# Another order for the start of a spectral-mixing and MoE kernel: weight loads behind a fold, spills on ScalarE's queue, step 0 earlier, a second warm-up, PSUM banks by name

## The chip, the cores and the metric

One core of a Trainium2 chip runs the whole kernel. The metric is the device time of one execution in microseconds (us), the median of several runs. The core has five engines that work beside each other, each through its own instructions in order: TensorE (PE; its weight loads are listed as PEld), VectorE (DVE), ScalarE (ACT), GpSimd (POOL) and SyncE (SP). SP computes nothing and issues DMAs; ScalarE issues some too. Each of the two has its own DMA queue, and both feed the same 16 DMA engines. Engines wait for each other and for DMAs through semaphores.

## The reference

```python
def _attn_ref(x):                       # x: (8, 3008, 256) float32
    X = np.fft.fft(x, axis=1)
    X = np.fft.fft(X, axis=2)
    return X.real.astype(np.float32)

def _moe_ref(x, w_in, w_out):           # w_in (256, 2048), w_out (2048, 256), float64
    h = x @ w_in
    g = h * (1.0 / (1.0 + np.exp(-1.702 * h)))
    return (g @ w_out).astype(np.float32)

x = _attn_ref(x).reshape(8 * 3008, 256); return _moe_ref(x, w_in, w_out)
```

A two-dimensional Fourier transform of each of 8 batches (its real part), then two matrix products with a sigmoid-weighted unit between.

## The kernel before, in words

The transform along the sequence (3008 = 47 * 64) is split into two stages of matrix products with tables of sines and cosines, `tab1` and `tab2`. The transform along the 256 columns is not done on the data: it is folded into `w_in` once, at the start (`fold_w`). What follows is `h`, its activation and the product with `w_out`, batch by batch, in 48 steps for each: a step is one (batch, block, half, p), with three blocks of transform rows, two halves of a block and eight pairs p of 128 rows of the hidden dimension, 16 steps a block.

**Start, batch 0 only.** x arrives in 48 rows and their mirror images: `load_first` on SP's queue and `load_mirror` on ScalarE's, four of each, in groups of four columns numbered 0 to 7 that arrive as the pairs (0, 7), (1, 6), (2, 5), (3, 4). DVE folds each group (`fold_first`, L310 and L312), PE mixes it into one PSUM bank (`mix_first`, L330, eight times), ScalarE copies the bank out to a buffer of `made` (L332). A buffer holds two mixes. `spill_first` (L336) writes the first 16 rows of a buffer to DRAM (`Td`) as soon as it is full, one DMA for each half c of the partitions; rows 16 to 48 follow later. `fill` (L358) reads `Td` back in the order that the second stage wants. `rotate` (PE into bank `psr`, ScalarE L365) mends one column, `stage2` (PE L378, DVE transposes L385) makes the tile `pq`, the operand of all steps of a block. So the first `pq` needs the last spill, then the fill, then `psr`.

**Weights.** `w_in` and `w_out` come as float64 in four chunks each of 1 MB (`load_in`, `load_out`), into a ring of three buffers, and are turned to float32 by hand: `sizes` (absolute value of the high word, ScalarE L429 or DVE L431), `clamp` (POOL L435), `low` (ScalarE L439), `high` (DVE L454 and L455), `finish_in` or `finish_out` (POOL L467 or L475). `bounds` is prepare, sizes, clamp and low together. `halved` (DVE L480, L481) adds and subtracts the halves of a chunk of `w_in`, and `fold_w` (PE L191 or L501 into `psw`, ScalarE L508) transforms the chunk. `first_row` (PE `psf`) and `nyquist` (PE `psn`) mend two rows.

**Steps 0 to 7** run by a hand-written list, `SCRIPT`: for each step `hidden` (PE `pa` and `pb`, ScalarE L552), then the entries of the step. `rows` (DVE L582, L587, L589) makes h of a step and frees the banks `pa` and `pb`, `activate` (ScalarE L593) the unit, `product` (PE `o`) the product with `w_out`. Steps 2n and 2n+1 of `hidden` use chunk n of `w_in`, and so do the products with `w_out`. From step 8 on another scheme with fewer products runs, the same in both kernels. `differences` (POOL L493) and `small_weights` (DVE L712) prepare its weights.

**What sets the order.** Each engine runs its instructions in the order in which the program names them. PSUM banks are handed out in turn from the list `spare`: a call takes the first name and puts it at the end, and PE waits where the bank's last reader isn't done. A DMA may also wait for an earlier one: eight completion semaphores serve all DMAs in turn. `warm` are matmuls without use that keep PE busy.

```python
spare = ["b0", "b1", "b2", "o2", "o3", "o4"]
```

Of the kernel before, what the change touches and what calls it, by code (L numbers as in the profile page):

```python
# [119 lines left out]
def kernel(ctx: ExitStack, tc, x, w_in, w_out, tab1, tab2, out):  # L120
# [213 lines left out]
    def spill_first(k, m0, m1, engines):  # L334
        for c, eng in enumerate(engines):
            eng.dma_start(out=view(Td[0], (NJ * m0 + 16 * c + 12 - 4 * k) * D, [NJ * D, m1 - m0], [1, 4 * D]),  # L336
                          in_=made[k][64 * c + m0:64 * c + m1].rearrange("p q d -> p (q d)"))
# [29 lines left out]
    def stage2(b, blk):  # L367
# [14 lines left out]
        for u in range(NU):  # L382
            for cs in range(parts):

                nc.vector.transpose(free(pq[:], cs * 512 + u * RUN, [256, 4 // parts], [NU * RUN, 4], [1, RUN]),  # L385
                                    free(ps[u][:], cs * 256, [128, 4 // parts], [32, 4], [1, 32]))
# [472 lines left out]
    made = rooms[:3] + [pqp.tile([128, 4, D], F32, tag="pq", name="e")[:]]  # L859
# [3 lines left out]

    nc.vector.memset(twos[:], 0.0)
    for lo, hi in (28, 32), (24, 28), (20, 24), (8, 12), (12, 20):
        nc.gpsimd.memset(xt[:, lo:hi, :], 0.0)
    nc.vector.memset(xt[:, 0:4, :], 0.0)
# [19 lines left out]
    load_in(0, nc.sync, ((0, 1), (1, 2)))  # L887
    nc.sync.dma_start(out=small[:, :CD + 4 * H], in_=tab2[:])
    load_in(1, nc.sync)
# [4 lines left out]
    for i, need in enumerate(((0, 7), (1,), (6,), (2,), (5,), (3,), (4,), ())):  # L894
        for g in need:
            fold_first(g)
        mix_first(i)
# [3 lines left out]
        if i % 2:  # L901
            spill_first(i // 2, 0, 16, (nc.sync, nc.scalar))
# [11 lines left out]
    load_out(0, nc.sync)  # L914
# [6 lines left out]
    sizes(in1, nc.vector)  # L921
    low(in1)
    for h0 in (0, 512):
        clamp(in1, h0, 512)
# [8 lines left out]
    halved(1)  # L933
# [7 lines left out]
    spare.append(spare.pop(0))  # L941
    high(out0)
    load_in(3, nc.sync)
    finish_out(0)
    fold_w(1)
# [11 lines left out]
    for t, c in ((1, 2), (3, 3)):  # L957
        at(t, load_out, c, nc.sync)
# [13 lines left out]
    for b in range(B):  # L972
# [26 lines left out]
        for blk in range(NBLK):  # L999
# [7 lines left out]
        [(prepare, in2), (low, in2), (nyquist, 0, 0), (rows, 0, ((sizes, in2, nc.vector), (clamp, in2)))],  # L1007
        [(first_row, 1), (activate, 0), (rows, 1), (high, in2), (finish, in2)],
        [(activate, 1), (rows, 2), (halved, 2)],
        [(product, 0, 0, None), (product, 1, 0, None), (bounds, out1), (activate, 2), (bounds, in3), (rows, 3), (activate, 3),  # L1010
         (fold_w, 2), (high, out1), (finish, out1), (high, in3), (finish, in3)],
        [(first_row, 2), (rotate, 0, 4, NG, nc.scalar.copy), (rows, 4), (halved, 3)],
# [103 lines left out]
```

## Time and profile before

| | |
|---|---|
| median of 3 runs | 1846.46 us (1846.12 to 1846.71) |
| profiled execution | 1845.24 us, span 1843.5 us |
| mean granted TensorE clock | 0.997 of full speed |
| ACT busy | 1139.4 us (62%) |
| POOL busy | 997.7 us (54%) |
| PE busy in the first 10 us, 10 to 20, 20 to 30, 30 to 40 | 7.44, 9.40, 8.09, 8.28 |
| DMA | 105.95 MB, mean 57 GB/s; 202 GB/s in the first 10 us, 277, 245 and 349 in the next three tens |

The profile is one execution taken by the hardware profiler. The span runs from the first to the last instruction; the execution's time has 1.7 us more around it. Busy times are per engine, and register, semaphore and DMA-issuing instructions don't count. "x<-y" names the tile written and the tile read; L336 is line 336 of the kernel before. SPq and ACTq are the engines' DMA issues. A line of the chain of waits has the start, the length and what it was. In a table of stretches, the granted clock stands behind the engines (1.00 is full speed).

### The profile page before, as it was taken

To read this page: it belongs to the slowest core of one execution; us is meant where nothing else is said; L and a number is where in the kernel's file an instruction comes from. 1 tells how busy PE (TensorE), PEld (TensorE's weight loads), DVE (VectorE), ACT (ScalarE), POOL (GpSimd) and SP (SyncE) were. 2 spreads that over 40 slices of the span, in tenths; PEclk is the share of its full clock that TensorE was granted. 3 is DMA by queue.
4 is the path that set the end of the run, shared out by engine and by line. 5 is a ranking of instruction groups with operands and counts; after the bars stand their busy time and mean duration, and the time that the engine had idled before them with its cause. 6 is when DMAs were issued, how large, how long until landed. Compare 5 with 4: busy or idle time off the path is not lost.

```text
span 1843.5 us, 55849 instructions
## 1 busy us (share of the span) xinstructions
PE 1826.2 (99%) x23650; PEld 1398.9 (76%) x23650; DVE 1479.1 (80%) x1930; ACT 1139.4 (62%) x2231; POOL 997.7 (54%) x1068
## 2 busy tenths in 40 slices
PE   8999999999999999999999999999999999999998
PEld 4677777777777777777777777777777877778776
DVE  6888788887888778877888778878888788878874
ACT  4666656666666666666666666666656666556663
POOL 3785555554656546564456644666446654444442
PEclk9999999999999999999999999999999999999999
DMA  8721331114211151211502115020241102100101
GB/s 276 189 70 26 90 65 28 55 32 106 43 48 40 35 112 30 61 35 45 111 13 73 33 50 97 23 72 26 75 74 28 29 26 59 28 19 13 23 19 24
DMA packets 150841, 105.95 MB, mean 57 GB/s; under 512 B 106197, under 2 KB 131799, under 8 KB 150032
## 3 DMA queue, kind: packets, MB, share of 16 engines
q1 hardware_dynamic: 147760, 100.33, 22.6%
q8 instruction: 186, 3.05, 0.7%
q10 hardware_dynamic: 2832, 2.05, 0.5%
q14 instruction: 63, 0.52, 0.1%
HBM read 65.07 MB, written 48.05 MB: 61 GB/s over the span
## 4 chain that ended last, share of the span: by engine, by line
PE 95%; POOL 2%; DMA 1%; DVE 1%; issue 0%; ACT 0%; ACTq 0%; DVEq 0%; POOLq 0%; SPq 0%
PE x L191 35%; PE o L191 26%; PE low L701 25%; PE o L701 4%; PE ps L268 2%; PE ps L378 1%; DMA xt<-in_x_dram 1%; PE po L191 0%; DMA big<-in_moe_w_in_dram 0%; PE psw L501 0%; POOL wo L475 0%; PE pa L191 0%; POOL wo L493 0%; POOL big L632 0%; DMA t<-Td 0%
## 5 line engine op out<-in xcount | busy, mean ns | idle before, releaser
L632 POOL TENSOR_TENSOR big<-big 128x256 f32<-128x256 f32 (+1 forms) x376 | 353.6, 940 | 785.7 <-ACT big L624 672.2
L191 PE MATMUL x<-pq,wcs 128*64 128x256 f32 (+1 forms) x6016 | 768.8, 376 | 1.5 <-ACT g L614 0.9
L191 PE MATMUL o<-big,wo 128*64 128x256 f32 (+1 forms) x4800 | 621.0, 375 | 0.5 <-DVE big L639 0.5
L191 PEld LDWEIGHTS x<-pq,wcs 128*64 128x64 f32 x6016 | 414.1, 137 | 181.4 <-issue 15.6
L614 ACT ACTIVATE g<-x 128x512 f32<-128x512 f32 (+1 forms) x376 | 221.7, 590 | 380.1 <-PE x L191 378.9
L191 PEld LDWEIGHTS o<-big,wo 128*64 128x64 f32 x4800 | 341.8, 137 | 146.8 <-DVE big L639 0.9
L633 POOL TENSOR_TENSOR big<-big 128x256 f32<-128x256 f32 (+1 forms) x376 | 411.2, 1094 | 0.0
L621 DVE TENSOR_TENSOR big<-g,x 128x512 f32<-128x512 f32 (+1 forms) x376 | 250.7, 667 | 183.6 <-ACT big L617 183.4
L602 ACT ACTIVATE x<-nb,af 128x256 f32<-128x256 f32 (+1 forms) x752 | 353.0, 469 | 70.1 <-DVE pq L385 57.0
L701 PE MATMUL low<-big 128*64 128x128 f32 (+1 forms) x5888 | 381.4, 270 | 0.0
L701 PEld LDWEIGHTS low<-big 128*64 128x64 f32 x5888 | 336.9, 137 | 28.2
L617 ACT ACTIVATE big<-x 128x512 f32<-128x512 f32 (+1 forms) x376 | 219.2, 583 | 122.2 <-PE x L191 112.2
L663 DVE TENSOR_TENSOR big<-big 128x1024 f32<-128x1024 f32 (+1 forms) x184 | 235.4, 1280 | 65.9 <-PE low L701 43.1
L624 ACT ACTIVATE big<-big 128x512 f32<-128x512 f32 (+1 forms) x376 | 231.6, 616 | 34.9 <-DVE big L621 32.6
L701 PE MATMUL low<-big,wo 128*64 128x128 f32 (+1 forms) x2944 | 220.3, 270 | 0.1
L665 DVE TENSOR_TENSOR big<-big 128x512 f32<-128x512 f32 (+1 forms) x184 | 179.6, 976 | 16.3 <-DVE big L663 0.5
L667 DVE TENSOR_TENSOR big<-big 128x512 f32<-128x512 f32 (+1 forms) x184 | 184.0, 1000 | 0.0
L701 PEld LDWEIGHTS low<-big,wo 128*64 128x64 f32 x2944 | 171.8, 137 | 4.2 <-DVE big L667 0.5
L640 DVE TENSOR_TENSOR big<-big 128x512 f32<-128x512 f32 (+1 forms) x188 | 143.3, 762 | 6.5
L639 DVE TENSOR_TENSOR big<-big 128x512 f32<-128x512 f32 (+1 forms) x188 | 131.2, 698 | 3.5 <-POOL big L632 3.5
L803 DVE TENSOR_TENSOR big<-big,low 128x512 f32<-128x512 f32 (+3 forms) x184 | 109.0, 609 | 3.8
L701 PEld LDWEIGHTS o<-big,wo 128*64 128x64 f32 x1472 | 92.3, 137 | 24.9
(104 smaller groups left out, 1100.5 us busy)
## 6 DMA issues: line engine op xcount, KB each, us to landing
out_dram<-os SPq DMA_DIRECT2D x284, 64.0 KB
t<-Td SPq DMA_DIRECT2D x22, 512.0 KB
Td<-xt SPq DMA_DIRECT2D x56, 192.0 KB
xt<-in_x_dram SPq DMA_DIRECT2D x14, 512.0 KB
xt<-Xr SPq DMA_DIRECT2D x14, 512.0 KB
nb<-Nd SPq DMA_DIRECT2D x23, 256.0 KB
out_dram<-os SPq DMA_DIRECT2D x96, 56.0 KB
Xr<-in_x_dram SPq DMA_DIRECT2D x7, 752.0 KB
```

Source lines behind the costliest of these rows:

```text
L191: nc.tensor.matmul(out[c0:c0 + 64], lhsT=lhs[:, c0:c0 + 64], rhs=rhs, skip_group_check=True, **how)
L602: nc.scalar.activation(x[:, i * 256:i * 256 + n], nbt[b, blk][:, hh * 256:hh * 256 + n], ACTF.Copy, scale=af1[:, f:f + 1])
L614: nc.scalar.activation(two(g[:], n), two(xb[t][:], n), ACTF.Copy, scale=2.0)
L617: nc.scalar.activation(front(t), two(xb[t][:], width(t)), ACTF.Gelu_apprx_sigmoid)
L621: nc.vector.tensor_tensor(back(t), two(gt.pop(t)[:], n), two(xb.pop(t)[:], n), op=ALU.subtract)
L624: nc.scalar.activation(back(t), back(t), ACTF.Gelu_apprx_sigmoid)
L632: eng.tensor_tensor(right(t, S1, n), left(t, A21, n), right(t, A22, n), op=ALU.add)
L633: eng.tensor_tensor(left(t, S3, n), left(t, A11, n), left(t, A21, n), op=ALU.subtract)
L663: nc.vector.tensor_tensor(free(big[:], SUM, *both_), free(big[:], from11 + w, *twice), free(big[:], from11, [at_right(t, 0) + w - from11, ...
L665: nc.vector.tensor_tensor(s2, a11, s1, op=ALU.subtract)
L667: nc.vector.tensor_tensor(s4, a12, s2, op=ALU.subtract)
L701: nc.tensor.matmul(o, lhsT=lhs, rhs=rhs, start=first_in, stop=(p == NP - 2), skip_group_check=True)
```

## The change

- `spill_first` can take several groups in one DMA. The first 16 rows of all buffers go on ScalarE's queue, behind mixes 1, 5 and 7 rather than 1, 3, 5 and 7, and the second and third buffer go together. To lie side by side, these two change places in `made`.
- The loads of `w_in`, chunks 0 and 1, and of `tab2` are issued by SP behind the fold of group 6 (the fourth fold, ahead of mix 2): a 4-byte store to DRAM reads what that fold wrote and stands ahead of them. `tab2` comes in two DMAs, the part for `fold_w` first. `load_out(0)` follows them at once; it stood behind the first `fill`.
- The sizes of `w_in`'s chunk 1 move from DVE (one instruction) to ScalarE (two halves).
- `halved(1)`, `high(out0)`, `load_in(3)`, `finish_out(0)` and `fold_w(1)` move from ahead of step 0 into step 0, behind its `hidden`. `stage2` transposes the cosine halves of both banks ahead of the sine halves.
- `warm(2)` stands ahead of `rotate`, and the banks from there on are named one by one in a list of 23.
- In `SCRIPT`, the entries of steps 0 to 3 are regrouped (chunk 2 of `w_in` is prepared over steps 0 to 2, chunk 3 is ahead of `w_out`'s chunk 1), and `load_out(2)`, `load_out(3)` stand behind the `high` that reads their buffer.
- One memset of x stands first on DVE.

```diff
-    def spill_first(k, m0, m1, engines):
+    def spill_first(k, m0, m1, engines, groups=1):
         for c, eng in enumerate(engines):
-            eng.dma_start(out=view(Td[0], (NJ * m0 + 16 * c + 12 - 4 * k) * D, [NJ * D, m1 - m0], [1, 4 * D]),
-                          in_=made[k][64 * c + m0:64 * c + m1].rearrange("p q d -> p (q d)"))
+            part = made[k][64 * c + m0:64 * c + m1]
+            eng.dma_start(out=view(Td[0], (NJ * m0 + 16 * c + 12 - 4 * k) * D, [NJ * D, m1 - m0], [1, 4 * groups * D]),
+                          in_=free(part, 0, [1, 4 * groups * D]))
...
-        for u in range(NU):
-            for cs in range(parts):
+        for cs in range(parts):
+            for u in range(NU):
...
-    made = rooms[:3] + [pqp.tile([128, 4, D], F32, tag="pq", name="e")[:]]
+    made = [rooms[0], rooms[2], rooms[1]] + [pqp.tile([128, 4, D], F32, tag="pq", name="e")[:]]
...
+    nc.vector.memset(xt[:, 0:4, :], 0.0)
     nc.vector.memset(twos[:], 0.0)
...
-    nc.vector.memset(xt[:, 0:4, :], 0.0)
...
-    load_in(0, nc.sync, ((0, 1), (1, 2)))
-    nc.sync.dma_start(out=small[:, :CD + 4 * H], in_=tab2[:])
-    load_in(1, nc.sync)
     warm(6)
...
+        if i == 2:
+            nc.sync.dma_start(out=Tk[0:1, :], in_=room[6][0:1, 0, 0:1])
+            load_in(0, nc.sync, ((0, 1), (1, 2)))
+            nc.sync.dma_start(out=small[:, CD:CD + 4 * H], in_=tab2[:, CD:])
+            nc.sync.dma_start(out=small[:, :CD], in_=tab2[:, :CD])
+            load_in(1, nc.sync)
+            load_out(0, nc.sync)
         mix_first(i)
...
-        if i % 2:
-            spill_first(i // 2, 0, 16, (nc.sync, nc.scalar))
+        if i in (1, 5, 7):
+            spill_first((0, 2, 3)[i // 3], 0, 16, (nc.scalar, nc.scalar), 1 + i % 3 // 2)
...
     fill(0, 0, 4)
-    load_out(0, nc.sync)
     load_in(2, nc.sync)
...
-    sizes(in1, nc.vector)
+    for h0 in (0, 512):
+        sizes(in1, nc.scalar, h0, 512)
+        clamp(in1, h0, 512)
     low(in1)
-    for h0 in (0, 512):
-        clamp(in1, h0, 512)
...
     fold_w(0)
-    halved(1)
+    spare[:] = ["b0", "o2", "b1", "b2", "b0", "o2", "o3", "o4", "b1", "b2", "o4", "o2", "b0", "o3", "b1", "b2", "b0", "b1", "o4", "o3",
+                "b2", "o2", "o4"]
+    warm(2)
     rotate(0, 0, 4, nc.scalar.copy)
...
     first_row(0)
-    spare.append(spare.pop(0))
-    high(out0)
-    load_in(3, nc.sync)
-    finish_out(0)
-    fold_w(1)
...
-    for t, c in ((1, 2), (3, 3)):
-        at(t, load_out, c, nc.sync)
...
     SCRIPT = (
-        [(prepare, in2), (low, in2), (nyquist, 0, 0), (rows, 0, ((sizes, in2, nc.vector), (clamp, in2)))],
-        [(first_row, 1), (activate, 0), (rows, 1), (high, in2), (finish, in2)],
-        [(activate, 1), (rows, 2), (halved, 2)],
-        [(product, 0, 0, None), (product, 1, 0, None), (bounds, out1), (activate, 2), (bounds, in3), (rows, 3), (activate, 3),
-         (fold_w, 2), (high, out1), (finish, out1), (high, in3), (finish, in3)],
-        [(first_row, 2), (rotate, 0, 4, NG, nc.scalar.copy), (rows, 4), (halved, 3)],
-        [(product, 2, 0, None), (activate, 4), (bounds, out2), (rows, 5), (activate, 5), (fold_w, 3), (high, out2), (finish, out2)],
+        [(nyquist, 0, 0), (halved, 1), (high, out0), (load_in, 3, nc.sync), (finish, out0), (prepare, in2),
+         (rows, 0, ((sizes, in2, nc.vector), (clamp, in2))), (fold_w, 1)],
+        [(activate, 0), (first_row, 1), (rows, 1)],
+        [(low, in2), (activate, 1), (high, in2), (load_out, 2, nc.sync), (finish, in2), (rows, 2)],
+        [(bounds, in3), (activate, 2), (prepare, out1), (sizes, out1, nc.scalar), (clamp, out1), (rows, 3), (activate, 3), (low, out1),
+         (halved, 2), (product, 0, 0, None), (product, 1, 0, None), (fold_w, 2), (high, in3), (finish, in3), (high, out1),
+         (load_out, 3, nc.sync), (finish, out1)],
+        [(first_row, 2), (rotate, 0, 4, NG, nc.scalar.copy), (halved, 3), (rows, 4)],
+        [(product, 2, 0, None), (activate, 4), (rows, 5), (bounds, out2), (fold_w, 3), (activate, 5), (high, out2), (finish, out2)],
...
-                spare[:] = [tag for tag in spare if tag[0] == "o"] + ["b2"]
+                spare[:] = ["o4", "o2", "o3", "b2"]
```

## The prediction

> **What bounds the kernel now.** The page first: PE is busy for 1826.2 of the span's 1843.5 us, and the chain that ended last is PE for 95%.
>
> ```profile
> PE 1826.2 (99%) x23650; PEld 1398.9 (76%) x23650; DVE 1479.1 (80%) x1930; ACT 1139.4 (62%) x2231; POOL 997.7 (54%) x1068
> ...
> PE 95%; POOL 2%; DMA 1%; DVE 1%; issue 0%; ACT 0%; ACTq 0%; DVEq 0%; POOLq 0%; SPq 0%
> ```
>
> From 100 to 1843 us PE is busy 1735.41 of 1743 us at full clock, and the change edits nothing there. So it can only shift the moment from which PE runs without gaps. The second view is the table of stretches over the start; its columns are the stretch, its length, the busy time of PE, PEld, DVE, ACT and POOL, the granted clock, the DMA share and GB/s.
>
> ```profile
> 22.00:26.00 4.00, 3.05 (x28) 1.56 (x25) 3.60 (x5) 2.40 (x5) 2.21 (x3) 1.00 0.92 362
> 26.00:28.00 2.00, 1.96 (x10) 0.48 (x8) 1.25 (x1) 1.19 (x1) 1.36 (x2) 1.00 0.03 10
> 28.00:30.00 2.00, 1.08 (x6) 0.14 (x2) 1.59 (x3) 1.17 (x2) 0.92 (x2) 1.00 0.49 89
> 30.00:32.00 2.00, 0.28 (x12) 0.29 (x17) 1.90 (x2) 0.00 (x0) 1.31 (x1) 0.97 1.12 440
> 32.00:36.00 4.00, 4.00 (x85) 2.82 (x86) 2.65 (x6) 2.07 (x3) 1.94 (x2) 0.50 0.99 378
> 36.00:40.00 4.00, 4.00 (x22) 1.68 (x20) 1.92 (x2) 2.08 (x7) 1.84 (x3) 0.66 0.75 274
> 59.00:61.00 2.00, 0.23 (x4) 0.00 (x0) 1.97 (x4) 0.58 (x1) 2.00 (x2) 1.00 1.02 383
> ```
>
> Three things are to be seen: the DMA engines are full until 26 and empty from 26 to 28; PE is idle around 30 and again at 59 to 61; and the clock is halved from about 31.9 (0.97 over two us) to about 38.7 (0.66 over four), nearly 7 us. Third, the chain of waits over the same place (start, length, what):
>
> ```profile
> 23.58 0.60 ACT e L332
> 24.20 3.17 DMA Td<-e
> ...
> 27.50 4.08 DMA t<-Td
> 31.59 0.14 issue
> 31.72 0.29 PE psr L191 x4
> 32.01 1.89 PE ps L378 x64
> 33.90 0.95 PE psf L191 x16
> 34.84 3.52 PE psw L501 x8
> 38.36 1.09 PE pa L191 x8
> ```
>
> The last spill of the first transform lands at 27.4, the read-back (`fill`) at 31.59, and only then can PE go on. From there PE is the chain. Last, what PE waits for between 24 and 100 us (total, times, longest):
>
> ```profile
> PE psr L191 <- DMA t<-Td: 2.6, 1, 2.6
> PE pb L191 <- DVE big L589: 1.9, 1, 1.9
> PE psw L191 <- POOL wst L467: 1.0, 1, 1.0
> PE pa L191 <- DVE big L589: 0.3, 1, 0.3
> ```
>
> **The change part by part**, in the profiled execution's time (span 1843.5, execution 1845.24; the median of the runs is 1846.46, so 1.22 are added at the end).
>
> *Weight loads behind the fold of group 6.* SP now waits for the DVE fold that starts at 15.00 and takes 0.69, then issues a 4-byte store (0.4), so the first `w_in` load is issued at about 16.1 instead of 14.92 (SP's timeline). Queued behind that wait on SP are both `w_in` loads, the tables and, new here, `load_out(0)`; the fill comes behind all of them. From issue to first data this queue took 2.0 us for that load and 1.3 for the fill, so weights flow from about 17.8. x's last pieces lose that rival: in the trace, the last fold that waits for x starts at 18.53. The gain for the folds is 0 to 1.0; I take 0.4. It doesn't reach the end of this stage, because ScalarE, which copies the results out, waits for the first `w_in` half (20.44 now, about 20 after) and now issues two spills of 0.36 each ahead of its last two copies, where it issued one. The last spills are issued at about 24.0 to 24.8 against 24.20: nothing.
>
> *Spills on ScalarE's queue behind a longer line of weights.* Bytes that must move from 17.8 on: 1.05 MB (w_in, chunk 0), 0.46 (tables), 1.05 (chunk 1), 1.05 (`load_out(0)`, formerly issued behind the fill at 27.93) and 0.52 of spills: 4.1 MB. The rows from 22 to 26 move 362 GB/s, the best slices inside them about 400. At 400 that is 10.3 us, so they end at 28.1, and 0.6 to 1.2 more pass until the slowest engine has counted its completion: the last spill lands at about 29.0 instead of 27.38. Bounds: it passes the weights because its queue is its own (about 27.1, by the 3.17 of the row above from an issue at 24.0), or comes behind everything at 362 GB/s (29.9). I take 29.0 for this reason: in this trace spills on ScalarE's queue did not pass. Issued at 19.63 and 22.70, they were complete at 24.94 and 27.06, 5.3 and 4.4 us later, among SP's spills issued at about the same times. Grouping two into one saves SP's and ScalarE's issue times (0.3 to 0.36 each), which hide in this wait. The fill then takes 4.08 with nothing ahead of it, as now: `psr` starts at about 33.2, **+1.5** (bounds -0.4 and +2.5).
>
> The Trainium skill (DMA: Bandwidth & Descriptors, "Queues, rings and completion order") has each DMA engine take turns between the queues packet by packet, by which the last spill would land near 27 and this term would be about -0.2. The two completions at 24.94 and 27.06 speak against that here.
>
> *Warm-up.* Two 128x512 matmuls (three took 2.84 at full clock, so 0.95 each) follow `fold_w(0)`, which ends at 29.1 once a bank is copied out: PE is busy to 31.0, then idle for 2.2 until `psr`. The trace has an idle of 2.64 (29.08 to 31.72), after which the clock fell, and one of 1.92 (59.23 to 61.15), at 1.00 throughout. 2.2 lies nearer to the second; I take it that the clock stays. The Trainium skill (TensorE: Matmul & The Clock Gate, "Why this matters for your kernels") asks for no idle over about 3 us. The 2.64 here shows that less is enough to lose the clock.
>
> *Step 0 ahead of `fold_w(1)`.* Before, from `psr` (31.72) to the end of step 1's `pb` (42.73) takes 11.0. After, at full clock: 0.2 and the second stage 1.1 (the same 64 rows took 1.19 at 84.10); hand-off 0.2; the first two of the four transposes 0.75, which the new loop order makes the ones `pa` needs, and which `psw` used to cover: 2.3. Then `pa`, `pb`, `psn` 0.87 each: 4.9; `psw` 1.72 (its row at 53.97): 6.6; `pa` 0.87: 7.5. Step 1's `pb` takes bank o2, which `rows(0)` frees. DVE gets there by the transposes (ready at 2.95), `halved(1)` 1.3, `high(out0)` 1.9, then L582, the sizes of in2, two L587 and L589 with 0.6 + 0.7 + 0.87 + 0.69: 9.0. So PE waits 1.5 and ends at 9.9: **-1.1**. With the clock halved, this part would lose about 1.8 (half of the 6.8 us, less what DVE's wait hides).
>
> *The waits behind it.* The 0.3 at 43.3 goes, since the banks are named so that `pa` of step 2 takes a free one: **-0.3**. The 1.9 at 59.2 is `pb` waiting for `rows(4)` to free its bank, with DVE behind a 2.18 us L455 that usually takes 1.23. The named bank removes the wait: at most -1.9. What is late next is the chain POOL finish, differences, clamp, DVE high and small weights, on the critical path from 59.97 to 85.9, while PE there has no gap. So part is given back: **-1.0** (bounds -1.9 and +1.4, the second from the rival below). `sizes(in1)` moves from DVE (1.25) to two ScalarE halves (0.7 each) ahead of the copies of `psw`, whose cover is the wait for the fill; `load_out(2)`, `load_out(3)` and `load_in(3)` change place behind DVE's `high`, which already released their buffers.
>
> Sum: +1.5 - 1.1 - 0.3 - 1.0 = -0.9, and -0.1 for the x memset put first on DVE: -1.0. 1845.24 - 1.0 + 1.22 = **1845.5**. A measurement of this kernel tells 0.2% (3.7 us) from no change.
>
> **The rivals.**
> *The clock falls all the same* in the idle before the late fill: -1.0 + 1.8 = +0.8, 1847.3. For it: 2.2 is also close to 2.64, and the second stage's small tiles may not count as work, since the clock stayed low through them from 32 to 36. Against it: the 1.92. Chance 0.25.
> *The spills pass the weights*, the engines taking the two queues in turn: the last lands near 27.1, the fill shares the engines with the rest of `load_out(0)`, and `psr` is at 31.5, so -1.0 - 1.7 = -2.7, 1843.8; with the whole 1.9 gained too, 1842.8. For it: the queue of spills holds nothing else by then. Against it: the two completions above. Chance 0.17.
> *POOL's finish of out1 is the new wait*, and the kernel ends slower. It now stands behind in3's finish: in3 2.36 and out1 3.85 in their slow rows, from about 56.2, end at 62.4, where PE would be ready for `product(2)` at 60.0. PE waits 2.4 and the 1.0 is lost: -1.0 + 3.4 = +2.4, 1848.9. It decides once that finish ends after about 61. Against it: at the usual 2.50, it ends at 61. Chance 0.10.
> *The change does nothing at the start* since the DMA total is the same: it isn't the same ahead of the fill, so this is within the first case.
>
> **How the numbers follow.** Forecast 0.48 (its own range 1843.8 to 1847.0, by the bounds of fill and later waits), clock 0.25, passing 0.17, POOL 0.10. Low end 1842.8, the passing case with the full gain; high end 1849.0, the POOL case, or a halved clock with the fill at +2.5. Over 3.7 us faster (below 1842.8) needs passing and every later gain: 0.10. Slower than 1850.2 needs two rivals together: 0.05. Within: 0.85.
>
> **What would show it.** Right: first `w_in` issue near 16.1; last spill landing near 29 and `psr` near 33; PEclk 1.00 from 32 to 40; 1.5 of PE idle before step 1's `pb` on L590 (the old L589); no idle of 1.9 near 59. Wrong: `psr` before 32 (spills pass), PEclk 0.5 after 33, or a wait of `o` on POOL's `wo` near 60. From 120 us on the two traces should keep one distance; if that grows, the cause is one I haven't named.

## The result, and the profile after

The changed kernel takes 1850.25 us (median of 17 runs, 1848.59 to 1851.61) against 1846.71 for the kernel before (17 runs beside it, 1845.42 to 1848.80): a ratio of 1.0018, 95% interval 1.0011 to 1.0026. It is 3.5 us slower, within the 0.2% that was called no change, but the interval leaves 1 out. The forecast was 1845.5, and 1850.25 lies above its range of 1842.8 to 1849.0.

The profiled execution took 1850.66 us with a span of 1848.6, so 5.1 more than the span of before. The page's first line and its chain:

```profile
PE 1828.8 (99%) x23654; PEld 1406.5 (76%) x23654; DVE 1480.1 (80%) x1929; ACT 1139.5 (62%) x2233; POOL 1000.2 (54%) x1068
...
PE 93%; DMA 2%; POOL 2%; DVE 1%; ACT 1%; issue 1%; SPq 0%; ACTq 0%; DVEq 0%; POOLq 0%
```

PE's share of the chain fell by 2 points, and DMA and ACT took some of it. The table of stretches over the start (stretch, length, busy time of PE, PEld, DVE, ACT and POOL, granted clock, DMA share, GB/s):

```profile
22.00:26.00 4.00, 3.62 (x44) 2.37 (x42) 3.93 (x6) 2.09 (x4) 2.19 (x3) 1.00 1.06 425
26.00:28.00 2.00, 1.84 (x8) 0.39 (x8) 0.40 (x1) 1.74 (x3) 0.97 (x1) 1.00 0.98 404
28.00:30.00 2.00, 1.64 (x8) 0.48 (x8) 1.05 (x2) 1.75 (x3) 1.46 (x3) 1.00 0.16 64
30.00:32.00 2.00, 2.00 (x6) 0.68 (x4) 1.97 (x3) 0.65 (x2) 1.31 (x1) 1.00 0.19 19
32.00:36.00 4.00, 1.43 (x53) 1.23 (x60) 0.47 (x1) 0.90 (x2) 1.26 (x1) 0.92 0.89 320
36.00:40.00 4.00, 4.00 (x60) 2.62 (x44) 3.21 (x7) 1.97 (x5) 1.04 (x1) 0.50 0.98 347
57.00:61.00 4.00, 2.88 (x20) 1.17 (x18) 3.03 (x2) 3.29 (x6) 3.70 (x2) 1.00 0.00 0
```

The DMA engines are now full until 28 instead of 26, and then nearly empty until 32: the pause of before is two us later and longer. PE is busy through 30 to 32, with the warm-up, but does 1.43 of the four us from 32. The clock is halved in 36 to 40 all the same. What PE waits for between 24 and 100 us:

```profile
PE psr L191 <- issue: 2.6, 1, 2.6
PE o L191 <- POOL wo L476: 1.6, 2, 1.1
PE x L191 <- ACT x L603: 1.4, 1, 1.4
PE pa L191 <- ACT wcs L509: 1.3, 2, 1.1
```

For `psr` the profile names no releaser ("issue"); by the time it is the fill, issued at 30.62. The 1.9 of `pb` on DVE and the 0.3 of `pa` are gone. In their place stand three waits on other engines, 4.3 us in sum. Adding up between moments that both traces have, in us (differences in the last column):

| | before | after | |
|---|---|---|---|
| `psr` starts | 31.72 | 34.78 | +3.06 |
| `psr` to `product(0)` | 15.34 | 15.07 | -0.27 |
| `product(0)` to `psw` of chunk 2 | 6.91 | 6.91 | 0 |
| `psw` of chunk 2 to `psw` of chunk 3 | 11.52 | 12.63 | +1.11 |
| `psw` of chunk 3 to the first `x` | 9.32 | 9.46 | +0.14 |
| first `x` to the 22000th PE row from the end | 83.83 | 85.40 | +1.57 |
| from there to the end of the span | 1684.86 | 1684.35 | -0.51 |

The sum is 5.1. The profiled execution of before (1845.24) lies 1.5 us under its median and that of after 0.4 above, so of the 5.4 between the two executions 3.5 are left between the medians. Two numbers of this table are used for every run below: the start of `psr`, and the way from `psr` to that 22000th row (126.92 before, 129.47 after), which says what the steps cost once the start is taken out.

### The profile page after: what moved, and what is told of

Its sections match the earlier page's. It is cut to its first block, busy times and chain, and to the rows that moved or that the text cites. A ratio compares the mean times of both kernels' runs of the same rounds, so it can differ in the third digit from the quotient of the medians.

```text
span 1848.6 us, 55856 instructions
## 1 busy us (share of the span) xinstructions
PE 1828.8 (99%) x23654; PEld 1406.5 (76%) x23654; DVE 1480.1 (80%) x1929; ACT 1139.5 (62%) x2233; POOL 1000.2 (54%) x1068
## 4 chain that ended last, share of the span: by engine, by line
PE 93%; DMA 2%; POOL 2%; DVE 1%; ACT 1%; issue 1%; SPq 0%; ACTq 0%; DVEq 0%; POOLq 0%
PE x L191 34%; PE o L191 26%; PE low L702 25%; PE o L702 4%; PE ps L268 2%; PE ps L379 1%; DMA big<-in_moe_w_in_dram 1%; DMA Td<-e 0%; DMA xt<-in_x_dram 0%; DMA wo<-in_tab_dram 0%; PE po L191 0%; POOL wo L476 0%; POOL wo L494 0%; POOL big L633 0%; DVE big L713 0%
## 5 line engine op out<-in xcount | busy, mean ns | idle before, releaser
L191 PE MATMUL o<-big,wo 128*64 128x256 f32 (+1 forms) x4800 | 627.8, 375 | 2.1 <-POOL wo L476 1.6
L191 PEld LDWEIGHTS x<-pq,wcs 128*64 128x64 f32 x6016 | 421.4, 137 | 178.1 <-issue 15.6
L191 PEld LDWEIGHTS o<-big,wo 128*64 128x64 f32 x4800 | 346.3, 137 | 147.4 <-POOL wo L476 2.6
L625 ACT ACTIVATE big<-big 128x512 f32<-128x512 f32 (+1 forms) x376 | 231.6, 616 | 37.0 <-DVE big L622 34.7
L702 PEld LDWEIGHTS low<-big,wo 128*64 128x64 f32 x2944 | 175.6, 137 | 3.9 <-DVE big L668 0.3
L702 PEld LDWEIGHTS o<-big,wo 128*64 128x64 f32 x1472 | 94.0, 137 | 24.3
```

Source lines behind the costliest of these rows:

```text
L191: nc.tensor.matmul(out[c0:c0 + 64], lhsT=lhs[:, c0:c0 + 64], rhs=rhs, skip_group_check=True, **how)
L625: nc.scalar.activation(back(t), back(t), ACTF.Gelu_apprx_sigmoid)
L702: nc.tensor.matmul(o, lhsT=lhs, rhs=rhs, start=first_in, stop=(p == NP - 2), skip_group_check=True)
```

## The experiments

Every kernel was timed against the kernel before on the same chip, in four groups of four; a ratio compares across groups better than a median. "Lists" is the kernel before with the new lists of the steps 1 to 5.

| edit | median us | ratio, 95% interval | `psr` | way |
|---|---|---|---|---|
| loads half only | 1847.78 | 1.0012, 1.0003 to 1.0020 | 34.29 | 126.78 |
| step half only | 1848.54 | 1.0015, 1.0005 to 1.0024 | 33.71 | 129.79 |
| after, memsets as before | 1849.27 | 1.0018, 1.0009 to 1.0027 | 35.16 | 128.04 |
| after, `load_out(0)` behind the fill | 1848.41 | 1.0013, 1.0004 to 1.0022 | 32.43 | 129.74 |
| before, spills only | 1845.48 | 0.9997, 0.9988 to 1.0006 | 32.53 | 127.90 |
| before, step 0 only | 1846.45 | 1.0001, 0.9992 to 1.0010 | 34.10 | 127.06 |
| before, lists of steps 1 to 5 only | 1850.99 | 1.0027, 1.0016 to 1.0038 | 31.97 | 132.66 |
| before, `warm(2)` only | 1845.69 | 0.9996, 0.9987 to 1.0005 | 33.34 | 127.91 |
| lists, out1 ahead of in3 | 1850.05 | 1.0020, 1.0011 to 1.0028 | 32.81 | 130.94 |
| after, out1 ahead of in3 | 1848.21 | 1.0012, 1.0004 to 1.0021 | 34.82 | 128.29 |
| after, out1 first, `load_out(0)` back | 1848.82 | 1.0013, 1.0005 to 1.0022 | 32.54 | 130.54 |
| before, spills and `warm(2)` | 1844.99 | 0.9996, 0.9987 to 1.0005 | 31.72 | 126.93 |
| lists, out1 first, `rows(4)` first | 1848.04 | 1.0009, 1.0000 to 1.0017 | 32.98 | 127.64 |
| after, `rows(4)` first | 1848.16 | 1.0011, 1.0002 to 1.0019 | 34.27 | 127.46 |
| after, steps 3 and 4 and `load_out(0)` as before | 1845.35 | 0.9994, 0.9986 to 1.0003 | 32.33 | 126.45 |
| before, spills, `warm(2)`, named banks | 1844.74 | 0.9994, 0.9985 to 1.0003 | 32.20 | 125.67 |

The last two columns are of one profiled execution each. When x's last pieces land varies by one or two us between executions, so a `psr` alone says less than the group of runs. In the seven kernels whose loads and first spills are those of before, `psr` starts between 31.72 and 34.10, mean 32.9, and the profile of before is the earliest of them. In the five with the loads and spills of the changed kernel it starts between 34.27 and 35.16, mean 34.7. By the groups the start is later by 1.7, not by the 3.06 of the one pair.

### The two halves

Each takes its lines of the change's diff, and leaves the others as before. *Loads half*: spills, loads behind the fold, memset, sizes of in1 (the diff down to `sizes(in1, nc.scalar, h0, 512)`, without the loop order in `stage2`). *Step half*: that loop order, `warm(2)`, named banks, step 0 and the lists.

> Only the loading half of the change: memset order, weight loads and load_out(0) behind the fold of group 6, spills on ScalarE's queue, sizes(in1) on ScalarE; the steps as before. Theory A (the loss is the late fill): psr near 34.8 against 31.72, and the whole loss is here, about +3 us against before (0 to +0.5 would refute it). Theory B (the loss is the new order of the steps): psr is as late, but the slack in the steps hides most of it: +1 us or less.

> Only the step half: transposes by cosine and sine, warm(2), named banks, halved(1), high(out0) and fold_w(1) inside step 0, the new lists of steps; the loads as before. Theory A: psr at 31.7 with no loss, 0 to -2 us against before, since warm(2) ends at about 31.0, the idle ahead of psr is under 1 us and the clock stays at 1.00. Theory B: PE still waits about 1.1 for ScalarE near 57, 1.7 for POOL near 62 and 1.3 for DVE near 88, and the kernel is +1 to +2 us slower than before.

Each half alone is slower: by 0.12% with a late `psr` (34.29) and the old way (126.78), and by 0.15% with a longer way (129.79). Both expectations missed in part. The loads half lost 1.7 us by the medians, between theory A's 3 and theory B's 1. The step half refutes theory A: it lost 2.5, a little above theory B's range, with waits of the kind that theory B names (2.4 on wcs, 0.9 on POOL, 1.3 on `x`), and the clock fell for 3.41 us behind an idle of 1.6. So two things had to be explained, a late start and dear steps.

### The late start: what stands ahead of the last spills

First the memset, whose new place also exchanges the completion semaphores: x's last load of `load_first` was issued at 11.62 in the changed kernel and at 7.98 before.

```diff
-    nc.vector.memset(xt[:, 0:4, :], 0.0)
     nc.vector.memset(twos[:], 0.0)
...
+    nc.vector.memset(xt[:, 0:4, :], 0.0)
```

> The changed kernel with the memset of x put back behind the others on DVE, nothing else. In the changed kernel x's last load on SP's queue was issued at 11.62 against 7.98 and landed at 19.56 against 16.40, because it now waits for the end of the table load. If the memset's place decides which earlier DMA it waits for: issue near 8, the last fold that waits for x about 1 us earlier, psr near 33.8 and about 1 us less than the changed kernel, +2.5 against before. If the DMA engines are the limit whatever the order: psr stays near 34.8 and +3.5 against before.

With the memsets back that load was issued at 7.81, but x's mirrors landed later instead (the last at 19.49) and `psr` came at 35.16. The order of x's loads isn't the cause; the DMA engines are full then.

Then `load_out(0)`:

```diff
-            load_out(0, nc.sync)
...
     fill(0, 0, 4)
+    load_out(0, nc.sync)
```

> The changed kernel with load_out(0) back behind the fill, nothing else. Theory A1 (spills wait behind all weights in one line): the last spill lands about 2 us earlier (28.3 against 30.48), psr near 32.7, 1.5 to 2 us less than the changed kernel. Theory A2 (the spills don't wait for load_out(0)): last spill and psr as in the changed kernel, 30.5 and 34.8, no gain.

`psr` came at 32.43, 2.35 earlier. The last two spills, issued at 25.07 and 25.42, landed at 27.83 and 27.98, under 2.8 us later. In the changed kernel this took 4.65 and 4.98. The other kernels agree: the last spill lands 4.8 to 5.2 us behind its issue in the five that have `load_out(0)` ahead of it, and 2.4 to 2.8 in the six that have the spills on ScalarE's queue and `load_out(0)` behind the fill. Two views of the changed kernel show it, SP's issues and the chain of waits (start, length, what):

```profile
15.92 0.83 SPq L412 DMA_DIRECT2D big<-in_moe_w_in_dram  x2
...
20.43 0.47 SPq L417 DMA_DIRECT2D big<-in_moe_w_out_dram  x1
30.62 0.38 SPq L359 DMA_DIRECT2D t<-Td  x1
```

```profile
25.15 0.31 ACTq L337
25.46 0.04 issue
25.50 4.97 DMA Td<-e
```

`load_out(0)` was issued 5 us ahead of the spills, and the fill (30.62) waited for the spills, which landed behind its megabyte. The spills on ScalarE's queue were tried by themselves, on the kernel before:

```diff
-    made = rooms[:3] + [pqp.tile([128, 4, D], F32, tag="pq", name="e")[:]]
+    made = [rooms[0], rooms[2], rooms[1]] + [pqp.tile([128, 4, D], F32, tag="pq", name="e")[:]]
...
-        if i % 2:
-            spill_first(i // 2, 0, 16, (nc.sync, nc.scalar))
+        if i in (1, 5, 7):
+            spill_first((0, 2, 3)[i // 3], 0, 16, (nc.scalar, nc.scalar), 1 + i % 3 // 2)
```

> The kernel before with one part of the change: the first spills all on ScalarE's queue, two groups in one DMA (and so the order of the made buffers). w_in, the tables and load_out(0) stay where they were (load_out(0) behind the fill), and the clock is not cared for. Theory A (of the loading half, load_out(0) ahead of the spills is what costs; the spills' new queue and form cost nothing): the fill is issued 2.4 to 3.2 us behind the last spill's issue, psr starts between 31.0 and 32.7, the time is 1845.5 to 1847.0, ratio 0.9995 to 1.0005. Rival B (one queue for all spills is itself the loss, for they land one behind the other): the last spill lands 4.5 us or more behind its issue with no load_out in its way, psr starts at 33.5 or later, the time is 1847.5 to 1848.5.

Here the last spill landed 2.5 us behind its issue (25.77 to 28.23), and the median came 1.1 below that of the kernel before, which the interval does not tell from 1. Theory A held, rival B fell.

But little of the 2.35 us came back as time: 1848.41, by the ratios 0.0005 (0.9 us) less than the changed kernel, with a way of 129.74. The chain of that kernel (`load_out(0)` behind the fill) says where the rest went, and two lines of its DVE timeline, with the idle time before them, say what DVE waited for:

```profile
30.20 9.68 DMA Td<-big
39.88 0.03 issue
39.91 0.05 DVEq L583
...
40.01 0.69 DVE big L583
40.70 0.69 DVE big L432
41.38 0.79 DVE dif L588 x2
...
42.94 1.11 PE pb L191 x8
```

```profile
37.43 0.69 DVE L455 TENSOR_SCALAR big<-big 128x1024 uint32<-128x1024 uint32 x1 [0.94 <-POOL big L436]
...
40.01 0.69 DVE L583 TENSOR_TENSOR big<-v,pb 128x512 f32<-128x512 f32 x1 [0.62 <-DMA Td<-big]
```

`rows(0)` (L583) writes h into a ring buffer that was one of the `made` buffers, and the later spill that still reads it lands at 39.88. PE waits 2.84 for `rows(0)`. However early `psr` is, `rows(0)` does not start before that spill has landed. DVE lost 0.94 more ahead of `high(out0)` (L455): it waits for POOL's clamp of `w_out`'s chunk 0, which is loaded later here. With `load_out(0)` early, as in the changed kernel, neither wait is there, so the early load costs some 2 us at the fill and saves part of them at step 0.

### Which part of the step half

Three kernels on the kernel before. Step 0 alone (with the named banks and `warm(2)`):

```diff
-    high(out0)
-    load_in(3, nc.sync)
-    finish_out(0)
-    fold_w(1)
...
-        [(prepare, in2), (low, in2), (nyquist, 0, 0), (rows, 0, ((sizes, in2, nc.vector), (clamp, in2)))],
+        [(nyquist, 0, 0), (halved, 1), (high, out0), (load_in, 3, nc.sync), (finish, out0), (prepare, in2), (low, in2),
+         (rows, 0, ((sizes, in2, nc.vector), (clamp, in2))), (fold_w, 1)],
```

> The kernel before with step 0 alone ahead of w_in's second transform (and the two warm-up products at psr that are named with it); all later steps in the order of before, low of in2 back in step 0. The step half as a whole cost 2.5 us. Theory A (that loss comes from the third step's list, where wcs copies and w_out's second finish come late): here TensorE has no new wait of over 0.4 near 58 to 66, the 1.9 wait ahead of step 5 stays, and the time is 1845.3 to 1847.3. Rival B (the loss is made at step 0: VectorE does halved(1) and high(out0) ahead of rows(0), so TensorE waits 1.4 to 2.8 for rows(0), and every later step is that much later): a wait of 1.3 or more between 40 and 45 on VectorE, and 1847.7 to 1848.8.

The lists alone (steps 2 to 5 as in the change's diff; these lines in the first two):

```diff
-        [(prepare, in2), (low, in2), (nyquist, 0, 0), (rows, 0, ((sizes, in2, nc.vector), (clamp, in2)))],
-        [(first_row, 1), (activate, 0), (rows, 1), (high, in2), (finish, in2)],
+        [(prepare, in2), (nyquist, 0, 0), (rows, 0, ((sizes, in2, nc.vector), (clamp, in2)))],
+        [(first_row, 1), (activate, 0), (rows, 1)],
```

> The complement: the kernel before with the new order of the steps 1 to 5 alone (in2's high and finish, load_out(2), list of step 3, fold_w(3)), step 0 and w_in's second transform as before, no warm-up at psr. Theory A (the third step's list costs): the 1.9 wait ahead of step 5 goes, and in its place TensorE waits 0.8 to 2.2 on ScalarE near 57 and 0.9 to 1.7 on POOL near 61 to 63, and 1.3 near 89; the time is 1847.5 to 1849.0. Rival B (step 0's order costs): those waits are under 0.5 in sum, the 1.9 is gained, and the time is 1844.5 to 1846.3.

The warm-up alone, which leaves the turn of the banks as it was:

```diff
     halved(1)
+    warm(2)
+    spare.insert(0, spare.pop())
     rotate(0, 0, 4, nc.scalar.copy)
```

> The kernel before with one edit: two 512-column products behind w_in's first transform, ahead of psr, in psr's own bank, so that TensorE idles some 0.9 us less there. It prices the clock by itself, which the profile of before shows at 0.5 from 31.87 for 6.83 us. Theory A (the clock pays at once): the granted clock stays 1.00 from psr on, psr to the end of step 1's pb shrinks from 11.0 to 9.0 to 10.2, and the time falls by 0.5 to 2.0: 1844.5 to 1846.2. Rival B (the clock gained at psr turns into a wait on VectorE or ScalarE, as at rows(0) where TensorE waited 2.8 with the clock at 1.00): psr to the 22000th row from the end keeps 126.9 within 0.4, and the time is 1845.9 to 1847.0.

Step 0 alone gives 1.0001 and the lists alone 1.0027: the loss of the step half is in the lists. With step 0 alone PE waited 0.84 for `rows(0)`, less than rival B's 1.3, and the way (127.06) is no shorter than that of before (126.92); the clock was at 0.5 for 3.41 us of it. Theory A missed one thing there: the 1.9 ahead of step 5 did not stay, for the named banks were part of this kernel, and a wait of 1.74 on ScalarE's wcs copies came at 68.19 in its place. The lists alone lost more than theory A had, 5.7 us of way: 2.27 on wcs, and the wait ahead of step 5, which was to go, stayed at 1.67, for the banks here are the old ones. After the first of the two the clock was granted at 0.5 for 10.24 us from 59.25. With `warm(2)` alone theory A missed on the clock (0.5 for 3.41 us from 35.54, behind an idle of 1.53, and again from 62.85) and rival B on the way (127.91). Its 0.9 us below the kernel before is inside the interval.

ScalarE's timeline in the kernel with the lists alone (start, length of the group, line, operation, idle before it and what ended that):

```profile
47.45 0.57 ACT L552 COPY v<-pa 128x512 f32<-128x512 f32 x1
51.48 1.19 ACT L429 ACTIVATE big<-big 128x1024 f32<-128x1024 f32 x1 [3.46 <-DMA big<-in_moe_w_in_dram]
52.56 1.29 ACT L439 ACTIVATE big<-big 128x1024 uint32<-128x1024 uint32 x1
53.76 1.04 ACT L593 ACTIVATE big<-big 128x1024 f32<-128x1024 f32 x1
54.70 1.19 ACT L429 ACTIVATE big<-big 128x1024 f32<-128x1024 f32 x1
55.80 1.04 ACT L593 ACTIVATE big<-big 128x1024 f32<-128x1024 f32 x1
56.74 1.11 ACT L439 ACTIVATE big<-big 128x1024 uint32<-128x1024 uint32 x1
57.76 1.04 ACT L508 COPY wcs<-psw 128x512 f32<-128x512 f32 x2
```

`bounds(in3)` comes first in step 3 now, and w_in's chunk 3 is only there at 51.48. ScalarE stands for 3.46, and queued behind are `activate(2)`, all of out1 and the two copies of `psw` that PE needs for `pa` of step 4. In the order of before, out1 (long loaded) filled that time, and ScalarE came to in3 at 50.73 with no wait. In the changed kernel the same chain ends in the new wait of 1.12:

```profile
42.01 10.92 DMA big<-in_moe_w_in_dram
52.93 0.02 issue
52.95 0.03 ACT big L430
...
58.16 1.07 ACT big L440
59.24 0.47 ACT wcs L509
59.71 0.04 issue
59.76 0.43 PE pa L191
```

### Out1 ahead of in3, and `rows(4)` ahead of `halved(3)`

```diff
-        [(bounds, in3), (activate, 2), (prepare, out1), (sizes, out1, nc.scalar), (clamp, out1), (rows, 3), (activate, 3), (low, out1),
+        [(bounds, out1), (activate, 2), (bounds, in3), (rows, 3), (activate, 3),
```

> The kernel before with the new order of the steps 1 to 5 (which cost 4.4 us), but in step 3 all of bounds(out1) ahead of bounds(in3), as before; everything else of the new lists stays. Theory A (the loss is ScalarE standing 3.5 us for w_in's chunk 3, which lands near 51.4, with the wcs copies and all of out1 queued behind it): ScalarE does sizes(out1) and low(out1) while chunk 3 is on its way, TensorE's wait of 2.3 on wcs near 56 to 58 falls under 0.5, the clock stays at 1.00 there, and the time comes back by 2.5 to 4.5 us to 1846.0 to 1848.5. Rival B (the loss is the rest of the lists: in2's low and high moved behind, halved(2) and halved(3) ahead of rows(4) on VectorE): TensorE loses as much in a wait on VectorE between 58 and 66, and the time stays at 1849.5 to 1851.5.

> The changed kernel with the same single edit: in step 3 all of bounds(out1) ahead of bounds(in3). Theory A: the wait of 1.12 on wcs near 58.6 and POOL's two of 1.05 and 0.60 ahead of product(2) fall to under 0.8 in sum, and the time falls by 1.5 to 3.0 against the changed kernel: 1846.5 to 1848.5. Rival B (the late fill and what follows it hold the end whatever the order in step 3): the waits move to the next step, and the time falls by under 0.7: 1848.8 to 1850.0.

> The changed kernel with both edits: out1's bounds ahead of in3's in step 3, and load_out(0) back behind the fill. Theory A (these two account for the whole loss): 1845.0 to 1847.0, no slower than the kernel before. Rival B (the early psr is again lost at rows(0), where TensorE waited 2.84 with load_out(0) behind the fill, and the clock with it): a wait of over 2 us between 40 and 43, and 1847.0 to 1848.5, as with step 3 alone mended.

The wait on wcs went in each or fell to 0.2, and the way became shorter by 1.72 with the lists alone and by 1.18 in the changed kernel: so ScalarE's stand is one cause. By the time, rival B was right on the first, 1850.05: TensorE lost as much on VectorE. In the second the time is theory A's (1848.21), but POOL's waits stayed, at 1.88. In the third rival B was right on the wait: the early `psr` (32.54) was lost at `rows(0)` again, where PE waited 2.85. The time, 1848.82, is 0.3 above its range. What was left stood in the first of the three, in DVE's timeline and PE's:

```profile
56.91 3.27 DVE L455 SCALAR_TENSOR_TENSOR big<-big 128x1024 uint32<-128x1024 uint32 x1
60.10 0.68 DVE L480 TENSOR_TENSOR big<-wst 128x512 f32<-128x512 f32 x1
60.71 1.74 DVE L481 TENSOR_TENSOR big<-wst 128x512 f32<-128x512 f32 x1
62.37 0.67 DVE L582 TENSOR_TENSOR big<-v,pb 128x512 f32<-128x512 f32 x1
```

```profile
64.70 1.97 PE L191 MATMUL pb<-pq,wcs 128*64 128x256 f32 x8 [4.84 <-DVE big L589]
```

`halved(3)` (L480, L481) now stands ahead of `rows(4)` and pushes it from 60.10 to 62.37. With the old banks PE waits for `rows(4)`, 4.84 where it was 1.92. So that pair was put back:

```diff
-        [(first_row, 2), (rotate, 0, 4, NG, nc.scalar.copy), (halved, 3), (rows, 4)],
+        [(first_row, 2), (rotate, 0, 4, NG, nc.scalar.copy), (rows, 4), (halved, 3)],
```

> The kernel before with the new lists of the steps 1 to 5, out1's bounds ahead of in3's as in the run that came out at 1.0020, and one more pair put back: in step 4 rows(4) ahead of halved(3). In that run TensorE waited 4.84 for rows(4) behind halved(3), which VectorE did at 60.10 to 62.4. Theory A (halved(3) ahead of rows(4) is the second half of the lists' loss): the wait falls to 2.0 to 2.8 and the time by 2.0 to 3.5, to 1846.2 to 1848.0. Rival B (the loss only moves: halved(3), now behind rows(4), makes w_in's last transform wait): a wait on VectorE of over 1.5 ahead of that transform near 66, and 1848.5 or more.

> The changed kernel with that pair alone put back: rows(4) ahead of halved(3). With its named banks no product waits for rows(4), so the gain must come by the longer way. Theory A (rows(4) late by 2.4 makes activate(4) late, and with it the bounds, high, finish of out2, the clamp and high of out3, rows(7), small_weights and the transposes in front of x): the wait of 1.35 on x near 91 falls under 0.5, the waits near 58 and 64 to 66 stay, and the time falls by 0.6 to 1.8 to 1848.0 to 1849.4. Rival B (that wait is made by the later start of everything, not by this order): it stays over 1.0, and the time within 0.5 of the changed kernel's 1.0018 to the kernel before.

With the lists alone the wait fell to 2.93 and the way by 3.30, and the time came to 1848.04; both lie a hair above theory A's ranges. Rival B's wait of over 1.5 ahead of the transform did not come: VectorE held that transform up for 0.6. The ways hold the clock too: from `psr` on it was at 0.5 for 17 us with the lists alone, for 10.2 with out1 first, and not at all with `rows(4)` first. As ratios the two pairs gave back 0.0007 and 0.0011 (1.3 and 2.0 us). In the changed kernel, whose banks let no product wait for `rows(4)`, the pair costs all the same: 1848.16, 2.1 below the changed kernel's median (in another group; as a ratio 0.0007 less), and the way 2.0 shorter. The wait on `x` near 90 fell from 1.35 to 0.50. Theory A's longer way is what happens: late `rows(4)`, late `activate(4)`, late out2, late out3, `small_weights` late on DVE, and the transposes that `x` needs stand behind them. What theory A had not: the waits on wcs and on POOL almost went too (0.4 left). In that execution PE had lost 2.4 ahead of `psw` at 24.5 and 1.8 at `rows(0)`, and so came later to both.

All put together, `load_out(0)` behind the fill, the two pairs, and in step 3 high and finish too:

```diff
-         (halved, 2), (product, 0, 0, None), (product, 1, 0, None), (fold_w, 2), (high, in3), (finish, in3), (high, out1),
-         (load_out, 3, nc.sync), (finish, out1)],
+         (halved, 2), (product, 0, 0, None), (product, 1, 0, None), (fold_w, 2), (high, out1), (load_out, 3, nc.sync),
+         (finish, out1), (high, in3), (finish, in3)],
```

> The changed kernel with load_out(0) back behind the fill and the lists of steps 3 and 4 in the order of before (out1's bounds, high and finish ahead of in3's, rows(4) ahead of halved(3)). Theory A (these lists and load_out(0) are the whole loss but for step 0): no wait over 0.5 between 55 and 95, the wait of 2.8 for rows(0) near 40 stays, and the time is 1845.5 to 1847.3. Rival B (TensorE's early start is paid back whatever the order, as VectorE, ScalarE and POOL have no time to spare between 50 and 90): waits of over 1.5 in sum come up there, and 1847.5 to 1849.

1845.35, 0.9994 (0.9986 to 1.0003), with the shortest way but one. With the lists of steps 3 and 4 and `load_out(0)` as before nothing is left of the loss, and the rest of the change shows no gain that the interval tells from none. What PE still waits for, in this kernel, between 24 and 100 us:

```profile
PE pb L191 <- DVE big L590: 2.8, 1, 2.8
PE x L191 <- ACT x L603: 1.9, 1, 1.9
```

So theory A holds but for the wait on `x`, which it had under 0.5: part of what the start gains is given back there.

### What the removed wait of 1.9 was worth

> The kernel before with the two parts that by themselves came out 1.1 and 0.9 us below it: the first spills all on ScalarE's queue with two groups in one, and two warm-up products ahead of psr. Theory A (the two are independent: the one brings the fill forward, the other the clock): 1844.0 to 1845.3, a ratio below 0.9995. Rival B (the gains of both are this measurement's noise, or the same gain counted twice): 1845.3 to 1846.8.

> The kernel before with the spills on ScalarE's queue, the two warm-up products, and named banks in its own order of steps, so that pb of step 5 takes a bank whose reader is long done: it prices the wait of 1.9 by itself, which the changed kernel was to remove. Theory A (removed in the old order of steps, the wait is worth what it took, less what x then waits): 1843.0 to 1844.6, a ratio of 0.9985 to 0.9994. Rival B (it is cover for VectorE and POOL alone, and comes back whole ahead of w_in's last transform or of x): 1844.6 to 1846.0, as without the named banks.

The first had 1844.99, 0.9996 (0.9987 to 1.0005), with an idle of 0.36 ahead of `psr` and the clock at 1.00 up to 60 us; the gain of theory A is possible and not shown. The second adds only named banks, in the order of steps of before:

```diff
+    spare[:] = ["b0", "o2", "b1", "b2", "b0", "o3", "o4", "o2", "b1", "b2", "o3", "o4", "b0", "o2", "b1", "b2", "o3", "b0", "b1",
+                "o4", "o2", "b2", "o3"]
...
-                spare[:] = [tag for tag in spare if tag[0] == "o"] + ["b2"]
+                spare[:] = ["o3", "b2", "o2", "o4"]
```

The wait of 1.9 on `rows(4)` went. In its kernel, between 55 and 95 us, this one came:

```profile
PE pa L191 <- ACT wcs L509: 1.7, 1, 1.7
```

It stands ahead of step 6, behind the copies of w_in's last transform. The way became 1.26 shorter, the medians differ by 0.25 and the ratios by 0.0002. With 1844.74 it lies inside rival B's range (from 1844.6), and with 0.9994 (0.9985 to 1.0003) at the edge of theory A's, so this run does not decide between them. It has the lowest median of all, 1.3 below the kernel before beside it, with an interval that still holds 1.

## Why the prediction was wrong

The forecast had the start 1.5 later and the way from `psr` 2.4 shorter (-1.1, -0.3 and -1.0). In the profiles the start was 3.06 later, 1.7 by the groups, and the way 2.55 longer. So the steps that failed are those of the way, the price of the later waits above all. Two rivals came true together, the clock and POOL's finish, to which the prediction gave 0.05.

*The fill, +1.5.* In the pair of profiles it was +3.06, above the bound of +2.5. There "the last spills are issued at about 24.0 to 24.8 against 24.20: nothing" failed: they were issued at 25.15 and 25.50, for x's last fold started at 19.68 and not at 18.53. The last landed at 30.48 for 29.0, and the fill took what it always does. But the profile of before was an early one: in the seven kernels with its loads and spills the last spill was issued between 23.69 and 25.70, in the five with those of the changed kernel between 24.76 and 25.98. By the groups the term is +1.7 and its size was right. What moves x's last pieces between executions is not settled. That spills don't pass the weights was right. The Trainium skill (DMA: Bandwidth & Descriptors, "Queues, rings and completion order") has the engines take turns between queues; here the spills took 4.65 and 4.98 us with `load_out(0)` ahead of them and 2.4 to 2.8 without. The sum had `load_out(0)` among its bytes, but did not single it out as the one that could stay away.

*The warm-up, "I take it that the clock stays".* It didn't: idle 2.58, then 0.5 from 35.34 for 6.83 us. The rival with chance 0.25 came true. The 1.92 that spoke against it lies just at the edge of what keeps the clock (see the last section).

*Step 0, -1.1.* From `psr` to the end of step 1's `pb` it took some 11.2, for 11.0 before and 9.9 forecast. The clock was halved for most of it and hides DVE's wait, as the rival had it. In the changed kernel with `rows(4)` first the clock stayed at 1.00 there: it took 10.4, with a wait of 1.82 in place of 1.5. So what failed in the changed kernel is the clock, and the sum was near. With `load_out(0)` back the clock stayed too, and it took 11.4, with a wait of 2.84. That "DVE gets there" as soon as its own work is done fails in that order: DVE waits 0.94 for POOL's clamp and 0.62 for the spill of the buffer that it writes.

*The waits behind, -0.3 and -1.0.* The 0.3 and the 1.9 went, as foreseen. "So part is given back: -1.0 (bounds -1.9 and +1.4)" failed: the table has +1.11 and +1.57 in this stretch. The edit was costed by the bank alone. That the lists also change the order on ScalarE (in3, not yet landed, ahead of out1) and on DVE (`halved(3)` ahead of `rows(4)`) was read as regrouping; on the lists alone the two pairs are 1.7 and 3.3 us of way, 1.3 and 2.0 us by the ratios. The POOL rival came true in its place (1.65 for 2.4), with another cause: POOL's finish of out1 started at 63.44, because out1's bounds came late and DVE's first `high` on it took 2.85, and it took 3.25:

```profile
59.19 2.85 DVE L455 TENSOR_SCALAR big<-big 128x1024 uint32<-128x1024 uint32 x1 [0.94 <-POOL big L436]
```

```profile
63.44 3.25 POOL L476 TENSOR_TENSOR wo<-big 128x512 uint32<-128x512 uint32 x2 [1.96 <-DVE big L456]
```

"Give back" by the chain through small weights came true as well, 1.35 at `x`.

*Where it was right*: the first `w_in` issue (15.92 for 16.1), no gain from the folds at the end of the stage, and one distance between the traces from about 100 us on (5.1 to 5.7 us).

## What to carry to other kernels

When a list of work for several in-order engines is rewritten, write down for each engine the order of before and after, and beside each entry when its data land: an entry whose data are 3 us away stops all that stands behind it on its engine. A large transfer moved ahead of a small one that the critical path waits for can hold it up on another queue too: here 1 MB kept 64 KB waiting for some 2.4 us. A wait removed by a free bank is worth only the distance to the next wait, here 1.3 of 1.9 in the way and 0.25 in the median, which is inside the noise. One profile of before is one draw: where a forecast starts from a moment that varies by two us between executions, look at several.

## What the runs showed of the hardware

The clock's loss does not follow from the length of the idle alone. In these profiles it was granted at 0.5 in pieces of 3.41 us or multiples of it. An idle of 2.58 cost 6.83 (the changed kernel) and one of 2.24 cost 3.41 (spills only). One of 1.92 cost nothing in the profile of before and 3.41 in that of the spills alone. One of 2.84 ahead of `pb` cost 3.41 with `load_out(0)` back, one of 2.85 cost 6.83 with out1 first as well, and one of 2.83 nothing with the lists of steps 3 and 4 back too. The Trainium skill (TensorE: Matmul & The Clock Gate, "What's actually happening") tells of a free-running window of 3.4 us.

The traces agree with such a window. In all 18 profiles the 60 changes of the granted clock after the first reading lie at whole multiples of 3.41 us from that reading. Cut into windows of that length, the first 100 us show how much idle of PE a window bears while the clock is at 1.00. All 11 windows with 1.94 us of idle or more were followed by 0.5, and so were 3 of the 7 with 1.81 to 1.92. Of the 433 with less, 7 were followed by 0.5, and each of these holds `psr` and the second stage's 64x32 matmuls. With `load_out(0)` back the idle of 2.84 fell into its windows as 0.78 and 2.06, with out1 first as well most of it (2.48) into one, and where it cost nothing as 1.91 and 0.92. So in these runs an idle of 2 to 3 us kept or lost the clock by where it fell in the windows, and that differs between executions.

DVE's second `high` instruction on 128x1024 elements takes 1.23 us and took 3.27 beside POOL's finish of in3 (the line at 56.91 above); its first, usually 0.69, took 2.85 in the changed kernel at 59.19, again beside that finish. The Trainium skill (GPSIMD Engine Reference, "8. Key points") has the two engines share their interfaces to SBUF and contend where the DVE instruction has two SBUF inputs, as the second has. The trace agrees for the second. The first has one SBUF input, and no run here shows why it was slowed. In these two places `high` beside a POOL finish cost DVE 2.0 and 2.2 us, where the prediction had one row of 2.18 to go by.
